# Keys of units 5 to 7 turned to token rows on VectorE instead of TensorE

## The chip, the cores and the metric

The kernel runs on one core of a Trainium2 chip. The metric is the device time of one execution in microseconds (us), taken as the median of several runs.

## The reference

A gated linear attention over 4 batches, 8 heads, 768 tokens and a head width of 48 feeds a three-way maxout layer of 3072 tokens, 384 inputs and 768 hidden features:

```python
f = 1 / (1 + np.exp(-f_logit))
for t in range(S):
    state = f[:, :, t, :, None] * state + np.einsum('bhd,bhe->bhde', k[:, :, t], v[:, :, t])
    y[:, :, t] = np.einsum('bhd,bhde->bhe', q[:, :, t], state)
x = y.transpose(0, 2, 1, 3).reshape(B * S, H * D)
h = np.maximum(np.maximum(x @ w1, x @ w2), x @ w3)
out = h @ w_out
```

Attention inputs are fp32, and the maxout weights come as 64-bit floats, so the kernel converts them to fp32 on the chip.

## The kernel before

**Units.** The sequence is cut into chunks of 64 tokens. A unit u is one chunk of two batches, 128 token rows, so there are 24 units, u = 0 to 23. A head is padded from 48 to 64 features, so two heads fill 128 partitions. For each unit the gates are scanned along the tokens (`scan`, line 316, and `before`, line 334). `after` makes kh, the keys times decay, with features on partitions (line 327), and `before` makes qh (line 338). `pairs` multiplies kh by qh into the PSUM tile a (line 379), and VectorE masks it into at (line 382). `values` multiplies at by v into the PSUM tile y (line 393), and then the keys by v into other columns of the same tile (line 402). For this second product the keys must stand with tokens on partitions, which is the tile ks. VectorE adds the product to the running state (line 410). `finish` adds the part of the older state into y (line 423), and ScalarE copies y to heads (line 429).

**Two ways to ks.** `keys(u)` makes ks with four 128x128 TensorE transposes into a PSUM tile tr (line 354) and one ScalarE copy (line 356). `keys_by_blocks(u, n)` makes one quarter of ks, 32 tokens, with four VectorE transposes that turn 32 by 32 blocks straight from kh to ks (line 369). It is called with n = 0 to 3 for each unit. Before the change, units 0 to 7 (`BY_ROWS = 8`) take the first way and units 8 to 21 the second; the last two units need no ks. The same constant also decides how f, k and q are loaded and turned to features: units 0 to 7 are loaded as token rows and turned by TensorE (line 278), later units are loaded in blocks and turned by VectorE (line 283).

**Maxout stage.** Four units make a group of 512 tokens. `pack` moves their heads to a tile xT by DMA (line 445). `ffn(g, xT)` is a generator. Each step multiplies one block of 128 hidden features by one of the three weights (line 472). The PSUM tile p, which has two buffers, is then read by ScalarE (line 477, for the first weight) or by VectorE (line 479, for the second into top and for the third into hm). After 18 such products come four output products (line 497) and their copies (line 500). A full step takes two turns of `fill`, and its instructions are issued in the first of the two. In the group g = 0, each step also issues conversion work for weights that are needed later: ScalarE (lines 228, 229, 232), then VectorE (line 242), then GpSimd (line 246).

**Order.** The schedule is written by hand. Every engine works through its own list in the order of the program text. `fill(n)` inserts n turns of the generator between the parts of a unit. The main loop runs over u from 4, and the part that matters reads:

```python
fill(...); keys(u); keys_by_blocks(u, 2); finish(u - 1); pairs(u)
sigmoids(u + 1); scan(u + 1)
fill(2); keys_by_blocks(u, 3); after(u + 1); before(u + 1)
fill(2); values(u); carry(u + 1)
fill(1 if u < 2 * GRP else 2)
keys_by_blocks(u + 1, 0)          # and one more fill here for u >= 8
keys_by_blocks(u + 1, 1)
```

Line numbers here and below are those of the profile. SP is the queue that issues nearly all loads and stores; its relevant lines are 182 (block loads), 163 (v), 445 (pack) and 505 (output).

Of the kernel before, what the change touches and what calls it, by code (L numbers as in the profile page):

```python
# [55 lines left out]
def kernel(  # L56
# [15 lines left out]
    NU = B // 2 * (S // C)  # L72
# [5 lines left out]
    GRP = 4  # L78
# [10 lines left out]
    def fast():  # L89
        ctx = ExitStack()  # L90
        with ctx:
# [58 lines left out]
            BY_ROWS = 8  # L150
# [196 lines left out]

            def keys(u):

                if u < min(BY_ROWS, NU - 2):  # L350
                    kh = ready[u]["kh"]
                    tr_s = ps_tr.tile([UT, HP, 128], FP32, name="tr")
                    for hp in range(HP):
                        nc.tensor.transpose(tr_s[:, hp, :], kh[:, hp].rearrange("p a t -> p (a t)"), ident)
                    ks = work.tile([UT, H, DP], FP32, name="ks")
                    nc.scalar.copy(ks.rearrange("s h d -> s (h d)"), tr_s.rearrange("s a d -> s (a d)"))
                    ready[u]["ks"] = ks

            def keys_by_blocks(u, n):

                if BY_ROWS <= u < NU - 2:
                    kh = ready[u]["kh"]
                    if n == 0:
                        ready[u]["ks"] = work.tile([UT, H, DP], FP32, name="ks")
                    ks = ready[u]["ks"].rearrange("s (hp par) d -> s hp par d", par=2)
                    a, t0 = divmod(n * 32, C)
                    for p0 in range(0, 128, 32):
                        par, e0 = divmod(p0, DP)
                        nc.vector.transpose(ks[n * 32:(n + 1) * 32, :, par, e0:e0 + 32], kh[p0:p0 + 32, :, a, t0:t0 + 32])  # L369
# [164 lines left out]
            with tc.manual_schedule():  # L534
# [13 lines left out]
                before(0)  # L548
                sigmoids(1)
                keys(0)  # L550
                scan(1)
                after(1)
# [3 lines left out]
                busy(1)  # L556
                values(0)
                keys(1)
                scan(2)
                after(2)  # L560
# [5 lines left out]
                busy(2)  # L566
                values(1)
                keys(2)
                scan(3)
                after(3)  # L570
# [41 lines left out]
                for u in range(GRP, NU):  # L612
                    n = u + 1
                    fill(0 if u == 2 * GRP else 4 if u % 2 and u > 2 * GRP else 2)
                    keys(u)
                    keys_by_blocks(u, 2)
                    if u > GRP:
                        finish(u - 1)
# [19 lines left out]
                    if CHECKS <= u < CHECKS + len(pieces) // 2:  # L638
                        check_range(2 * (u - CHECKS))
                    fill(2)  # L640
                    keys_by_blocks(u, 3)
                    if n < NU:
                        after(n)
# [13 lines left out]
                    if BY_ROWS <= u + 2 < NU and u % GRP == 0:  # L657
                        load(u + 2, one, "q")
                    keys_by_blocks(n, 0)
                    if u >= 2 * GRP:  # L660
                        fill(2)
# [267 lines left out]
```

## Time and profile before

| | |
|---|---|
| median of 13 runs | 478.95 us (476.82 to 482.94) |
| profiled execution, device time | 481.26 us |
| its span, first to last instruction | 479.6 us |
| TensorE busy | 458.0 us |
| VectorE busy | 269.1 us |
| ScalarE busy | 146.0 us |
| GpSimd busy | 111.1 us |

The span is the part that the trace shows; the profiled execution took 1.66 us more than that and is 2.31 us above the median. In the profile PE is TensorE's matmuls, PEld its weight loads, DVE VectorE, ACT ScalarE, POOL GpSimd. A name such as `tr<-ident,kh` gives the tile written and the tiles read. In the chain of waits each line is a start, a length and a piece of work, all in us.

### The profile page before, as it was taken

What the parts mean: (1) busy time and instruction counts of PE and PEld (TensorE: products, weight loads), DVE (VectorE), ACT (ScalarE), POOL (GpSimd) and SP (SyncE); (2) the same over time, 40 slices, a digit from 0 to 9 for tenths busy, and PEclk for the clock granted to TensorE, in tenths of its full rate; (3) what the DMA queues carried; (4) which work ended last, traced back from release to release, by engine and by line L of the source; (5) the groups of instructions that cost most, each with busy time, mean ns of one, the idle gap of its engine ahead of it and who ended that gap; (6) DMA issues with size and microseconds to landing.
All of it is one profiled execution on the core that took longest, in us unless ns stands there. A gap on an engine that the chain in (4) does not pass through costs nothing.

```text
span 479.6 us, 10276 instructions
## 1 busy us (share of the span) xinstructions
PE 458.0 (96%) x4063; PEld 248.5 (52%) x4063; DVE 269.1 (56%) x528; ACT 146.0 (30%) x343; POOL 111.1 (23%) x134
## 2 busy tenths in 40 slices
PE   4979899999999999999999999999999999999995
PEld 3757645556445445545445544455554445444453
DVE  5965776767487584487685568684674320021110
ACT  2443467522012234144233243242343211100000
POOL 2283644441231230330330311330311300000000
PEclk9987999999999999999999999999999999999999
DMA  9996998614467444576534477524470011200002
GB/s 133 134 287 176 212 347 120 93 49 64 99 95 104 128 81 114 94 138 81 157 77 117 83 139 88 161 62 97 105 146 9 1 51 39 45 1 0 2 17 52
DMA packets 175637, 47.92 MB, mean 100 GB/s; under 512 B 155136, under 2 KB 173184, under 8 KB 175584
## 3 DMA queue, kind: packets, MB, share of 16 engines
q1 hardware_dynamic: 170016, 42.50, 45.8%
q0 software_dynamic: 1008, 3.54, 2.4%
q10 hardware_dynamic: 4560, 1.18, 1.5%
q8 instruction: 33, 0.54, 0.5%
q14 instruction: 20, 0.16, 0.1%
HBM read 37.75 MB, written 4.72 MB: 89 GB/s over the span
## 4 chain that ended last, share of the span: by engine, by line
PE 77%; SPq 8%; DMA 6%; DVE 3%; issue 2%; ACT 2%; ACTq 1%; DVEq 0%
PE p L472 50%; PE p L497 17%; SPq L182 4%; DMA f_ld<-in_f_logit_dram 3%; PE y L423 2%; PE y L393 2%; DMA k_ld<-in_k_dram 2%; PE y L402 2%; SPq L505 2%; PE a L379 2%; DMA raw<-in_moe_w_dram 1%; PE tr L278 1%; SPq L163 1%; DVE r L316 1%; ACTq L445 1%
## 5 line engine op out<-in xcount | busy, mean ns | idle before, releaser
L472 PE MATMUL p<-xT,w_in 128*128 128x512 f32 (+1 forms) x684 | 293.7, 581 | 4.1 <-DVE top L479 2.2
L472 PEld LDWEIGHTS p<-xT,w_in 128*128 128x128 f32 x684 | 128.5, 193 | 139.9 <-issue 127.1
L497 PE MATMUL p<-w_out,hm 128*128 128x384 f32 x288 | 96.3, 489 | 0.0
L479 DVE TENSOR_TENSOR top<-p,top 128x512 f32<-128x512 f32 (+1 forms) x38 | 24.9, 656 | 107.5 <-PE p L472 107.5
L497 PEld LDWEIGHTS p<-w_out,hm 128*128 128x128 f32 x288 | 54.0, 190 | 37.6 <-issue 1.9
L369 DVE STREAM_TRANSPOSE ks<-kh 32x128 f32<-32x128 f32 x224 | 67.7, 302 | 3.6
L477 ACT COPY top<-p 128x512 f32<-128x512 f32 (+1 forms) x38 | 21.3, 562 | 151.4 <-PE p L472 151.4
L326 POOL COPY ends<-r 128x8 f32<-128x8 f32 x24 | 6.9, 288 | 188.2 <-DVE r L316 188.2
L479 DVE TENSOR_TENSOR hm<-p,top 128x512 f32<-128x512 f32 (+1 forms) x38 | 24.7, 651 | 30.5 <-PE p L472 30.5
L429 ACT COPY heads<-y 64x256 f32<-64x256 f32 (+1 forms) x72 | 26.6, 369 | 46.0 <-PE y L423 44.6
L327 POOL TENSOR_TENSOR kh<-kt,r 128x512 f32<-128x512 f32 x16 | 31.4, 1960 | 36.5 <-DVE kt L283 26.1
L500 ACT COPY o<-p 128x384 f32<-128x384 f32 x24 | 11.4, 476 | 86.8 <-PE p L497 83.0
L316 DVE TENSOR_TENSOR_SCAN r<-gate,from_one 128x520 f32<-128x520 f32 x24 | 29.8, 1240 | 9.7 <-ACT gate L295 5.7
L334 DVE TENSOR_TENSOR_SCAN prod<-gate,from_inv 128x520 f32<-128x520 f32 x24 | 31.0, 1291 | 0.0
L246 POOL TENSOR_TENSOR w_in<-top_bits,rest_bits 128x384 uint32<-128x384 uint32 x18 | 19.3, 1076 | 27.5 <-DVE top_bits L242 15.9
L382 DVE TENSOR_TENSOR at<-a,mask 128x512 f32<-128x512 f32 x24 | 16.6, 690 | 11.6 <-PE a L379 11.2
L393 PEld LDWEIGHTS y<-at,v_ld 64*64 64x64 f32 x768 | 13.4, 134 | 15.5 <-issue 9.7
L344 POOL TENSOR_TENSOR state<-st,ends 128x384 f32<-128x384 f32 x22 | 19.8, 901 | 0.1
L338 POOL TENSOR_TENSOR qh<-qt,prod 128x512 f32<-128x512 f32 x16 | 18.8, 1178 | 4.2 <-DVE qt L283 4.2
L283 DVE STREAM_TRANSPOSE gate<-sig 128x512 f32<-128x512 f32 x16 | 11.3, 705 | 15.0 <-ACT sig L298 15.0
L423 PEld LDWEIGHTS y<-qh,state 48*48 48x48 f32 x704 | 11.7, 123 | 13.8 <-issue 11.6
L393 PE MATMUL y<-at,v_ld 64*64 64x64 f32 x768 | 16.7, 224 | 0.0
(79 smaller groups left out, 307.9 us busy)
## 6 DMA issues: line engine op xcount, KB each, us to landing
raw<-in_moe_w_dram SPq DMA_DIRECT2D x27, 384.0 KB, 4.9
v_ld<-in_v_dram SPq DMA_DIRECT2D x48, 96.0 KB, 3.5
raw<-in_moe_w_out_dram SPq DMA_DIRECT2D x12, 384.0 KB, 6.3
out_dram<-o SPq DMA_DIRECT2D x47, 96.0 KB, 2.2
raw<-in_moe_w_dram POOLq DMA_DIRECT2D x9, 384.0 KB, 7.7
xT<-heads SPq DMA_DIRECT2D x30, 72.0 KB, 2.1
f_ld<-in_f_logit_dram SPq DMA_DIRECT2D x32, 64.0 KB, 2.7
k_ld<-in_k_dram SPq DMA_DIRECT2D x32, 64.0 KB, 2.6
```

The source lines that it names most:

```text
L316: nc.vector.tensor_tensor_scan(r[:, 0:LEN][:, ::-1], flat(gate)[:, ::-1], flat(from_one)[:, ::-1], 1.0, op0=ALU.mult, op1=ALU.max)
L327: (nc.vector if u < BY_ROWS else nc.gpsimd).tensor_tensor(kh.rearrange("p h a t -> p a h t"), kt, by_batch(r[:, 1:LEN + 1].rearrange("p (x ...
L334: nc.vector.tensor_tensor_scan(flat(prod), flat(gate_tiles[u % 2]), flat(from_inv[u % 2]), 1.0, op0=ALU.mult, op1=ALU.max)
L344: nc.gpsimd.tensor_tensor(t, states[u % 2], ends[:, u, :].unsqueeze(2).to_broadcast([128, 2 * HP, D]), op=ALU.mult)
L369: nc.vector.transpose(ks[n * 32:(n + 1) * 32, :, par, e0:e0 + 32], kh[p0:p0 + 32, :, a, t0:t0 + 32])
L393: nc.tensor.matmul(y[o:o + DP, a, hp * C:(hp + 1) * C], lhsT=v_ld[s, 2 * hp + par, :], rhs=d["at"][s, par, hp, :], start=(hp == 0), stop=F ...
L423: nc.tensor.matmul(y[o:o + D, a, hp * C:(hp + 1) * C], lhsT=st[r, a, hp, :], rhs=d["qh"][r, a, hp, :], start=False, stop=(hp == HP - 1), s ...
L429: nc.scalar.copy(heads[o, :, t0 + a * C:t0 + (a + 1) * C], y[i, a, 0:HP * C].rearrange("p (h t) -> p h t", h=HP))
L472: nc.tensor.matmul(p if g or w < TOK else p.rearrange("p (two t) -> p two t", two=2), lhsT=w_in[i][:, kt, j * 128:(j + 1) * 128], rhs=rhs, ...
L477: nc.scalar.copy(top, p)
L479: nc.vector.tensor_tensor(hm[:, j, t] if i == 2 else top, p, top, op=ALU.max)
L497: nc.tensor.matmul(p[:, 0:DM], lhsT=hm[:, j, i * UT:(i + 1) * UT], rhs=w_out[:, j, :], start=(j == 0), stop=(j == NJ - 1))
```

## The change

For units 5, 6 and 7 ks is now made by `keys_by_blocks` on VectorE and no longer by `keys` on TensorE and ScalarE. Unit 4 stays as it was, because its first two quarters would be due in the turn u = 3, which the loop does not have. `BY_ROWS` stays 8, so loads and the turning of f, k and q are untouched. GRP is 4 and NU is 24.

```diff
             def keys(u):
 
-                if u < min(BY_ROWS, NU - 2):
+                if u < min(GRP + 1, NU - 2):
                     kh = ready[u]["kh"]
                     tr_s = ps_tr.tile([UT, HP, 128], FP32, name="tr")
...
             def keys_by_blocks(u, n):
 
-                if BY_ROWS <= u < NU - 2:
+                if GRP + 1 <= u < NU - 2:
                     kh = ready[u]["kh"]
                     if n == 0:
                         ready[u]["ks"] = work.tile([UT, H, DP], FP32, name="ks")
```

## The prediction

> **What bounds the kernel now.** I read the busy shares first, then the forms of the two kinds of key transposes.
>
> ```profile
> PE 458.0 (96%) x4063; PEld 248.5 (52%) x4063; DVE 269.1 (56%) x528; ACT 146.0 (30%) x343; POOL 111.1 (23%) x134
> ...
> L354 PE MATMUL tr<-ident,kh 128*128 128x128 f32 x32 | 5.5, 297 | 0.4 <-DVE kh L327 0.4
> ...
> L369 DVE STREAM_TRANSPOSE ks<-kh 32x128 f32<-32x128 f32 x224 | 67.7, 302 | 3.6
> ```
>
> Over the whole span TensorE is the bound and VectorE is little over half busy. Line 354 runs 4 times for each of 8 units; line 369 runs 16 times for each of 14 units. But the change touches only units 5 to 7, so next I read the chain of waits there, and the windows.
>
> ```profile
> 84.77 0.44 PE tr L354 x4
> 85.20 0.59 PE y L423 x32
> 85.80 0.47 PE a L379 x32
> ...
> 108.07 0.52 PE y L402 x31
> ...
> 108.69 0.57 DVE st L410
> ...
> 109.30 0.66 PE y L423 x32
> ```
>
> From 62.65 to 108.59 us the chain holds TensorE alone, and the transposes of units 5, 6 and 7 stand in it at 72.80, 84.77 and 99.30 us, 0.44 us each. At 108.6 it goes over VectorE: finish(7) (line 423) has no product between it and values(7), and waits until line 410 has read the same PSUM tile.
>
> ```profile
> 72.60:84.60 12.00, 12.00 (x163) 6.99 (x162) 8.10 (x13) 8.47 (x18) 4.99 (x6) 1.00 0.80 116
> 84.60:99.10 14.50, 14.50 (x169) 8.13 (x168) 9.51 (x13) 7.55 (x16) 7.59 (x8) 1.00 0.55 77
> 99.10:109.30 10.20, 9.42 (x151) 5.72 (x150) 7.06 (x11) 2.80 (x6) 3.71 (x4) 1.00 0.25 63
> ```
>
> The columns are length, then busy PE, PEld, DVE, ACT, POOL. VectorE is busy 24.67 of these 36.7 us, so only 12.0 us are free. Its waits from 70.2 to 109.3 us are these:
>
> ```profile
> DVE at L382 <- PE a L379: 4.1, 3, 2.4
> DVE r L316 <- ACT gate L295: 4.0, 2, 2.0
> DVE top L479 <- PE p L472: 2.2, 1, 2.2
> DVE st L410 <- PE y L402: 1.3, 1, 1.3
> ```
>
> They are slack: TensorE loses nothing to them except at line 410.
>
> [...] a block transpose moves 32x128 in 302 ns, while line 283 moves 128x512, sixteen times the data, in about 700. [...] scans (two inputs) stretch beside GpSimd, block transposes do not, as the timeline of VectorE shows.
>
> ```profile
> 92.07 1.72 DVE L334 TENSOR_TENSOR_SCAN prod<-gate,from_inv 128x520 f32<-128x520 f32 x1
> ...
> 105.56 1.20 DVE L334 TENSOR_TENSOR_SCAN prod<-gate,from_inv 128x520 f32<-128x520 f32 x1
> ...
> 109.16 3.76 DVE L369 STREAM_TRANSPOSE ks<-kh 32x128 f32<-32x128 f32 x12
> ...
> 121.55 2.50 DVE L369 STREAM_TRANSPOSE ks<-kh 32x128 f32<-32x128 f32 x8
> ```
>
> Twelve take 3.76 us and eight 2.50, both partly beside GpSimd: 0.3125 us from start to start.
>
> **The change part by part.**
>
> *Removed on TensorE:* 3 units x 0.44 us = 1.32 us, all on the path.
>
> *Removed on ScalarE:* 3 copies of 0.58 us (line 356). They stand ahead of the copies to heads and of the next gate, which come about 0.46 us earlier from them and 0.44 from TensorE. ScalarE is off the path, so I price this at nothing by itself; its cover is that TensorE never waits for it here.
>
> *Freed:* one PSUM tile tr per unit. In this stretch line 278 waited for it only once (0.3 us, for the copy of unit 4, which stays). Nothing.
>
> *Added on VectorE:* 3 x 16 = 48 transposes x 0.3125 = 15.0 us, against 12.0 us free. So VectorE fills up and becomes the bound. No DMA and no instruction on SP or POOL is added or moved. Where it is late, POOL is late too (weight sums, line 246; kh and qh of unit 8), and TensorE through at, kh, qh, ks and the two buffers of p.
>
> To see where lateness lands I walk VectorE's list through the new order, each instruction at its start-to-start time in this trace. B8 is two quarters (2.50 us), B4 one (1.25).
>
> Unit 5: line 242 of the step before ends at 71.36; B8 to 73.86; line 242 to 74.32; B4 to 75.57; at (0.69) to 76.26, where it began at 74.37 before. The gate of unit 6 is ready at 76.6, so VectorE idles 0.35 us, its last pause. Then scan and reciprocal 1.39, top 0.57, line 242 twice 0.93: 79.50. B4 to 80.75; kh 0.60, second scan 1.16, qh 0.61, hm 0.60, line 242 0.46, state 0.47: 84.65. TensorE reaches the keys' product (line 402) at 81.1, after ks is whole: no wait.
>
> Unit 6: B8, line 242 (0.50), B4, at: 89.59 instead of 87.02. Scan and reciprocal 1.40, top 0.56, line 242 0.47, B4: ks of unit 6 is whole at 93.27. TensorE, by now 0.88 us ahead, wants it at 92.62 and **waits about 0.7 us**. kh, scan, qh, hm, line 242, state (0.60, 1.16, 0.61, 0.59, 0.47, 0.47): 97.17. hm frees p at about 96.3, just as TensorE wants it.
>
> Unit 7: line 242 blocked by GpSimd as now (1.17), B8, top 0.60, B4, at 0.69, gate, scan and reciprocal 2.15: 105.53. hm ends at about 106.15, when the output product wants it: just in time. B4 to 107.34, then unit 8's kt, scan and qt (0.62, 1.12, 0.68): 109.76. Line 410 runs behind them, to 110.35. So **finish(7) starts at 110.39 instead of 109.30**. GpSimd turns the late kt and qt into qh of unit 8 by 111.28, so pairs(8) starts at 111.33 instead of 109.96: **1.37 us late**, with the 1.32 us of TensorE work already given back.
>
> In this walk the second scans of units 6 and 7 take 1.16 us instead of 1.55 and 1.82, and one line 242 takes 0.50 instead of 1.17, because GpSimd's work no longer falls beside them: 1.72 us less. That is the least certain term. Bounds: all of it comes (the walk), or none of it does, and the result is 1.7 us later. Below the walk there is little: the counted instructions have no slack left but 0.35 us. I take the walk.
>
> *What is absorbed:* at 141.3 TensorE waits about 0.45 us for q of unit 10, at the end of a row of SP issues that runs without a break from 101 us, begun by heads(6), which the change does not delay. A late TensorE does not meet this wait: 1.37 - 0.45 = +0.92 us. Later stretches over SP and ScalarE (183, 264 us) start from TensorE's own results, so the rest passes through to the end.
>
> Span 479.6 + 0.92 = 480.5; with the 1.66 us around it the profiled execution would be 482.2. That execution is 2.31 us above the median, so against the median: 478.95 + 0.92 = **479.9 us**.
>
> **The rivals.**
>
> *A, GpSimd's relief does not come* (slower): VectorE, full from 76.6 us on, pays the contended times. Line 410 of unit 7 then ends near 112, and finish(7) and pairs(8) with it: +0.92 + 1.72 = +2.6, 481.6 us. It decides for slower as soon as 0.5 us more than in the walk falls on VectorE. For it: all pauses are used up, so each such delay counts fully. Against: scans outside this stretch do run at 1.12.
>
> *B, VectorE hides everything*: -1.32, 477.6 us. It needs the 48 transposes to fit into 12.0 us, so 0.25 us each; no row shows them so short.
>
> *C, the gain is made and lost at 141 us*: if VectorE costs nothing and SP's row does not move, TensorE arrives early and waits: 478.95. That SP's row starts from heads(6), which would be earlier too, speaks against it.
>
> That the change does nothing is excluded by the code: for units 5 to 7 all four quarter calls exist, and unit 4 keeps its own way.
>
> **How the numbers follow.** A difference under 0.3%, or 1.44 us, is about what a measurement of this kernel cannot tell from none. Walk: 0.50 (of which 0.08 ends above 480.4, 0.42 within). A: 0.35, slower. C: 0.08, same. B: 0.07, since -1.32 lies just inside the bound, 0.02 same and 0.05 faster with a little help. Faster 0.05, same 0.52, slower 0.43. The range 478.0 to 482.0 leaves out most of B, and the upper part of A where new contention joins.
>
> **What would show it.** Right: VectorE without pauses from 76 to 110 us; line 382 of unit 6 near 89; a TensorE wait of under 1 us for ks of unit 6 near 93; finish(7) near 110.4 after a wait for line 410 of about 2.4 us (0.7 before); line 356 five times, line 369 272 times. Wrong: pauses of VectorE left in unit 7 (B or C), second scans of units 6 and 7 still at 1.5 to 1.8 us or finish(7) after 111.5 (A), or a long TensorE wait at the p buffers, which in the walk come free just in time.

## The result and the profile after

The changed kernel takes 483.01 us (median of 11 runs, 480.26 to 484.47), the kernel before 479.16 us in the same comparison (48 runs). The recorded ratio is 1.0072, with a 95% interval of 1.0049 to 1.0094: slower by 3.4 us (2.3 to 4.5). The two medians are 3.85 us apart, which lies within that interval. Slower is the side that 0.43 was given to; 483.01 us lies above the predicted 479.9 us and above the range of 478.0 to 482.0. The profiled execution took 483.89 us, with a span of 482.2.

The page of the changed kernel, busy times and the granted TensorE clock in tenths, and then the clock on the page of before:

```profile
PE 458.5 (95%) x4051; PEld 247.3 (51%) x4051; DVE 282.9 (59%) x576; ACT 144.6 (30%) x340; POOL 107.6 (22%) x134
...
PEclk9988999997999999999999999999999999999999
```

```profile
PEclk9987999999999999999999999999999999999999
```

VectorE has its 48 instructions more and 13.8 us more work. The new thing is the 7 in the tenth slice (108.5 to 120.5 us), where the page of before has a 9. The low third and fourth slices stand in both. The windows of the changed kernel, columns as before:

```profile
72.60:84.60 12.00, 11.25 (x150) 6.14 (x138) 11.52 (x25) 8.45 (x19) 3.65 (x5) 1.00 0.82 116
84.60:99.10 14.50, 14.23 (x164) 7.77 (x164) 14.00 (x31) 6.32 (x14) 5.50 (x7) 1.00 0.52 72
99.10:109.30 10.20, 9.43 (x147) 5.27 (x146) 9.79 (x23) 2.22 (x5) 2.00 (x4) 1.00 0.28 68
```

VectorE is now busy 35.31 of 36.7 us. Of its waits from 70.2 to 109.3 us none is left: the only one that the view lists for this window, 0.7 us ahead of hm, was over at 69.79 us. TensorE waits instead. Its timeline in the changed kernel (start, length, line, idle time ahead and what ended it):

```profile
84.70 0.66 PE L423 MATMUL y<-qh,state 48*48 48x64 f32 x32 [0.85 <-DVE st L410]
...
93.35 0.66 PE L402 MATMUL y<-v_ld,ks 64*64 64x48 f32 x26 [0.17 <-DVE ks L369]
...
110.69 0.66 PE L423 MATMUL y<-qh,state 48*48 48x64 f32 x32 [2.17 <-DVE st L410]
111.76 1.13 PE L379 MATMUL a<-qh,kh 48*64 48x64 f32 x32 [0.40 <-POOL qh L338]
112.82 10.70 PE L497 MATMUL p<-w_out,hm 128*128 128x384 f32 x24
```

These are finish(5), the key product of unit 6, finish(7), pairs(8) and the two output products behind it. The same last three in the kernel before:

```profile
109.30 0.66 PE L423 MATMUL y<-qh,state 48*48 48x64 f32 x32 [0.78 <-DVE st L410]
109.78 0.65 PE L379 MATMUL a<-qh,kh 48*64 48x64 f32 x32
110.36 8.01 PE L497 MATMUL p<-w_out,hm 128*128 128x384 f32 x24
```

The waits at finish(5), at the key product and at finish(7) are VectorE's lateness. The lengths of the last two lines are something else: pairs(8) took 0.65 us and the two output products 8.01, here 1.13 and 10.70. The windows of the changed kernel show why. After PEld, DVE, ACT and POOL, the third number from the end is the granted clock:

```profile
110.70:111.70 1.00, 0.66 (x32) 0.51 (x32) 0.96 (x4) 0.28 (x1) 1.00 (x2) 0.88 0.03 2
111.70:113.00 1.30, 1.24 (x33) 1.12 (x34) 1.25 (x5) 0.83 (x3) 0.80 (x2) 0.50 0.00 0
...
117.00:118.00 1.00, 1.00 (x3) 0.50 (x2) 0.96 (x2) 0.00 (x0) 0.00 (x0) 0.50 0.68 86
118.00:119.00 1.00, 1.00 (x4) 0.63 (x3) 0.94 (x3) 0.00 (x0) 0.19 (x1) 0.86 0.55 64
```

From about 111.5 to 118.3 us TensorE got half its clock.

To compare stages, I take starts from the timelines of TensorE, counted from values(4) (its first line 393), because the stretch from the start to values(4) takes 64.2 to 67.4 us in the fourteen profiles, whatever the kernel. Each column is the time from the point before it:

| profile of | values(4), from start | to finish(7) | to pairs(8) | to values(8) | to finish(8) | to finish(11) | to finish(15) | to finish(19) |
|---|---|---|---|---|---|---|---|---|
| before | 66.31 | 42.99 | 0.48 | 8.52 | 12.87 | 50.64 | 72.80 | 74.30 |
| before, again (e12) | 64.88 | 42.99 | 0.48 | 8.52 | 12.87 | 50.73 | 72.99 | 72.02 |
| changed | 65.83 | 44.86 | 1.07 | 11.69 | 12.87 | 50.16 | 72.47 | 72.60 |
| changed, again (e5) | 66.57 | 44.87 | 1.07 | 10.07 | 12.87 | 50.16 | 72.04 | 72.11 |

So the change makes TensorE 1.87 + 0.59 = **2.46 us late** at pairs(8), the same in both executions. The clock adds 3.17 us in one and 1.55 in the other. About 0.5 us comes back before finish(11), where TensorE no longer waits for a load.

### The profile page after: what moved, and what is told of

Same layout as the page of the kernel before. It is cut to its first block, busy times and chain, and to the rows that moved or that the text cites. A ratio compares the mean times of both kernels' runs of the same rounds, so it can differ in the third digit from the quotient of the medians.

```text
span 482.2 us, 10295 instructions
## 1 busy us (share of the span) xinstructions
PE 458.5 (95%) x4051; PEld 247.3 (51%) x4051; DVE 282.9 (59%) x576; ACT 144.6 (30%) x340; POOL 107.6 (22%) x134
## 4 chain that ended last, share of the span: by engine, by line
PE 82%; DVE 7%; DMA 5%; issue 2%; SPq 1%; POOL 1%; ACT 0%; DVEq 0%; ACTq 0%; POOLq 0%
PE p L472 52%; PE p L497 20%; DMA k_ld<-in_k_dram 2%; PE y L393 2%; PE y L423 2%; PE a L379 2%; PE y L402 2%; DVE r L316 2%; DVE ks L369 1%; DVE prod L334 1%; SPq L182 1%; DMA f_ld<-in_f_logit_dram 1%; DMA q_ld<-in_q_dram 1%; POOL kh L327 1%; DMA raw<-in_moe_w_dram 1%
## 5 line engine op out<-in xcount | busy, mean ns | idle before, releaser
L497 PE MATMUL p<-w_out,hm 128*128 128x384 f32 x288 | 99.2, 500 | 0.0
L369 DVE STREAM_TRANSPOSE ks<-kh 32x128 f32<-32x128 f32 x272 | 82.2, 302 | 4.4
L497 PEld LDWEIGHTS p<-w_out,hm 128*128 128x128 f32 x288 | 55.2, 195 | 39.4 <-issue 5.2
L326 POOL COPY ends<-r 128x8 f32<-128x8 f32 x24 | 5.6, 233 | 191.6 <-DVE r L316 191.6
L246 POOL TENSOR_TENSOR w_in<-top_bits,rest_bits 128x384 uint32<-128x384 uint32 x18 | 18.3, 1018 | 26.7 <-DVE top_bits L242 16.1
L393 PEld LDWEIGHTS y<-at,v_ld 64*64 64x64 f32 x768 | 13.4, 134 | 15.5 <-issue 10.2
L283 DVE STREAM_TRANSPOSE gate<-sig 128x512 f32<-128x512 f32 x16 | 11.3, 705 | 13.8 <-ACT sig L298 13.8
L423 PE MATMUL y<-qh,state 48*48 48x64 f32 x704 | 14.6, 221 | 3.7 <-DVE st L410 3.7
```

The source lines that it names most:

```text
L393: nc.tensor.matmul(y[o:o + DP, a, hp * C:(hp + 1) * C], lhsT=v_ld[s, 2 * hp + par, :], rhs=d["at"][s, par, hp, :], start=(hp == 0), stop=F ...
L423: nc.tensor.matmul(y[o:o + D, a, hp * C:(hp + 1) * C], lhsT=st[r, a, hp, :], rhs=d["qh"][r, a, hp, :], start=False, stop=(hp == HP - 1), s ...
L497: nc.tensor.matmul(p[:, 0:DM], lhsT=hm[:, j, i * UT:(i + 1) * UT], rhs=w_out[:, j, :], start=(j == 0), stop=(j == NJ - 1))
```

## The experiments

**Theories.** *Clock*: the loss is VectorE's lateness plus a fall of the granted clock that TensorE's pauses at finish(7) and pairs(8) bring about. *Lateness alone*: the fall is chance, or belongs to something else, and the lateness accounts for the loss. A second question is where the lateness comes from: VectorE filled up (15.0 us into 12.0), or each moved unit costing by itself. The table gives each run against the kernel before on the same chip, with the mean granted clock of its runs. The clock of the kernel before is 0.9915 in the sets of e1 to e8 and 0.9910 in that of e9 to e12. In the first comparison only the 13 executions of the changed kernel have clocks on record, so their 0.9876 can be set only against the later sets.

By estimate 0.001 of mean clock is 0.5 us (0.001 x 480). But the mean takes in the whole span. In all fourteen profiles TensorE is also slow between 30 and 42 us: the windows show 0.50 from 32 to 41 us in the kernel before and 0.52 from 33 to 40 in the changed one, and in the others two products of 128x256 take 1.19 us there, or sixteen to nineteen take 5.29 to 7.49, where e12 has two in 0.70 just before and the kernel before has twelve in 2.75 at a clock of 1.00. Behind the last product, where it costs no time, the windows have 0.79 from 478.0 to 479.5 us in the kernel before and 0.52 from 480.0 to 482.2 in the changed one. So small differences of the mean say little, and only profiles show where the clock falls.

| run | ratio, 95% interval | mean clock | values(4) to finish(7), us |
|---|---|---|---|
| changed, first comparison | 1.0072 (1.0049 to 1.0094) | 0.9876 | 44.86 |
| e5 changed, again | 1.0072 (1.0051 to 1.0092) | 0.9885 | 44.87 |
| e1 changed, pause filled | 1.0053 (1.0027 to 1.0078) | 0.9918 | 44.87 |
| e2 before, 9 more on VectorE | 1.0040 (1.0022 to 1.0058) | 0.9890 | 44.40 |
| e3 before, 8 fillers on TensorE | 1.0028 (1.0009 to 1.0048) | 0.9926 | 45.80 |
| e8 before, 15 more on VectorE | 1.0091 (1.0068 to 1.0113) | 0.9860 | 46.40 |
| e4 changed, output product moved | 1.0089 (1.0056 to 1.0123) | 0.9865 | 46.70 |
| e6 units 5 and 6 only | 1.0034 (1.0020 to 1.0048) | 0.9920 | 43.68 |
| e7 unit 7 only | 1.0033 (1.0019 to 1.0047) | 0.9896 | 43.01 |
| e9 changed, VectorE lightened | 0.9997 (0.9976 to 1.0018) | 0.9907 | 41.95 |
| e10 before, VectorE lightened | 0.9987 (0.9963 to 1.0012) | 0.9914 | 42.99 |
| e11 before, one filler | 0.9984 (0.9967 to 1.0001) | 0.9917 | 42.99 |

### e1: the changed kernel with the pause filled

`busy(n)` issues n filler products whose result nobody reads (line 523); the kernel before already has such products in its first units.

```diff
+                    if u == 2 * GRP:
+                        busy(4)
                     if u > GRP:
                         finish(u - 1)
```

> The changed kernel, with four filler products (line 523, result unused, about 2.1 us) on TensorE between values(7) and finish(7), where it would wait for VectorE. Clock theory: the 2.2 us wait made the granted clock fall to 0.50 for about 7 us, which cost 3.1 us; with TensorE kept busy the clock stays at 1.00, finish(7) and pairs(8) start as in the changed kernel (within 0.3 us), the two output products behind them take 8.0 us instead of 10.7, and the time is 0 to 1 us above the kernel before (ratio 1.000 to 1.002). Lateness theory: the loss comes from VectorE's late results alone and the clock was chance; the time stays where the changed kernel is, 1.005 to 1.009.

The timeline of TensorE in e1:

```profile
108.84 1.99 PE L523 MATMUL p<-from_one,ident 128*128 128x256 f32 x8
111.08 0.66 PE L423 MATMUL y<-qh,state 48*48 48x64 f32 x32 [0.24 <-DVE st L410]
112.15 0.69 PE L379 MATMUL a<-qh,kh 48*64 48x64 f32 x32 [0.41 <-POOL qh L338]
112.77 8.01 PE L497 MATMUL p<-w_out,hm 128*128 128x384 f32 x24
```

The filler stands where the pause was. finish(7) and pairs(8) come as late after values(4) as in the changed kernel (44.87 and 1.07 us), yet the output products are back at 8.01 us, and the mean clock over twelve runs is that of the kernel before. So the clock follows the pause and not the late data. The time is 1.0053, outside the 1.000 to 1.002 that I expected of the clock theory and just inside the 1.005 to 1.009 written for lateness alone. The first range had taken off 2 us for a wait at 288 us that turned out to be chance (e12). Lateness without any fall of the clock, 2.46 - 0.5 = 2.0 us, is 1.004, inside the interval. By times e1 and the changed kernel are not apart, since their intervals overlap; it is the clock that differs.

### e5: the changed kernel again

No edit.

> The changed kernel once more, unaltered, to see how often and where the granted clock falls. Clock theory: the mean granted clock of its runs lies below that of the kernel before by 0.003 to 0.004 (1.5 to 2 us of 480), the drop lies behind the wait at finish(7), and the time is 2.3 us of lateness plus that, ratio 1.006 to 1.010. Lateness alone: the mean clocks are equal and the ratio is about 1.005, as with the filler in e1_warm.

The waits repeat to 0.01 us, and the clock falls at the same place, for a shorter time. TensorE in e5:

```profile
112.51 1.13 PE L379 MATMUL a<-qh,kh 48*64 48x64 f32 x32 [0.40 <-POOL qh L338]
113.58 9.07 PE L497 MATMUL p<-w_out,hm 128*128 128x384 f32 x24
```

Within this set the clock of the six runs is 0.0030 below before, 1.4 us. Over the 19 runs of the changed kernel it is 0.0036 below the same value, 1.7 us, as expected, and the ratio is 1.0072 again.

### e2, e8 and e3: the kernel before made late by pausing and by working

In e2 and e8, n = 9 and 15 unused block transposes go ahead of line 410 of unit 7; in e3 eight fillers go ahead of finish(7), as in e1.

```diff
+                    if u == 2 * GRP - 1:
+                        scratch = work.tile([128, PIECE], FP32, name="top_bits", bufs=4)
+                        scratch = scratch[0:32, 0:128].rearrange("p (x t) -> p x t", t=32)
+                        for i in range(n):
+                            nc.vector.transpose(scratch, ready[u]["kh"][0:32, :, 0, 0:32])
                     values(u)
```

> The kernel before, with nine more VectorE block transposes (line 369's kind, into an unused tile, 2.8 us) between unit 8's qt and the state of unit 7 (line 410); keys still by TensorE. This makes TensorE wait about 2.2 us at finish(7) instead of 0.7 and changes nothing else. Clock theory: the granted clock falls to 0.5 for about 7 us, TensorE is 1.5 + 3.1 = 4.6 us late at 123 us, of which about 2.4 us is absorbed later; time +2 us or more, ratio 1.004 to 1.007. Lateness theory: +1.5 us at most, clock at 1.00, ratio 1.000 to 1.003.

> The kernel before, with eight filler products (about 4.2 us, result unused) on TensorE between values(7) and finish(7). TensorE is late by 4.2 - 0.7 = 3.5 us there without having paused. Absorption theory: TensorE waits 0.45 us near 141 and 2.0 us near 288 us for loads anyway, and both waits shrink by what it is late: time +1.0 us, ratio 1.001 to 1.003, with the wait near 288 us gone. Pass-through, as the prediction had it: 3.5 - 0.45 = +3.0 us, ratio 1.006. In both the clock stays at 1.00.

> The kernel before, with fifteen more VectorE block transposes (4.7 us, into an unused tile) between unit 8's qt and line 410 of unit 7. TensorE waits about 4.0 us at finish(7), so it is about 3.4 us late there, as late as with the eight fillers of e3_busy8, but idle instead of working. Clock theory: the granted clock falls to 0.5 for some us in most runs, mean clock lower than before by 0.004 or more, time above e3_busy8's by about 3 us: ratio 1.009 to 1.013. Lateness alone: same as e3_busy8 within its interval plus the difference in lateness, ratio 1.003 to 1.006, clock as before.

The windows of e8, which waited 4.18 us at finish(7), and then those of e3:

```profile
108.00:114.00 6.00, 1.82 (x82) 1.28 (x84) 5.51 (x19) 0.48 (x1) 2.71 (x3) 1.00 0.32 60
114.00:118.00 4.00, 4.00 (x68) 2.67 (x58) 3.83 (x12) 1.10 (x3) 0.00 (x0) 0.57 0.04 10
```

```profile
108.00:114.00 6.00, 6.00 (x84) 4.44 (x83) 3.79 (x12) 1.11 (x3) 0.00 (x0) 1.00 0.21 28
114.00:118.00 4.00, 4.00 (x13) 2.31 (x13) 1.73 (x2) 1.00 (x2) 0.00 (x0) 1.00 0.47 70
```

TensorE is 3.41 us late at finish(7) in e8 and 2.81 in e3, nearly the same. But in e8 it had paused, and its clock was then 0.57 on average from 114 to 118 us; in e3 it had worked, and it stayed at 1.00. Over all runs the mean clocks are 0.9860 and 0.9926, a difference of 3.2 us, and the times differ by 1.0091 - 1.0028 = 0.0063, 3.0 us, of which 0.6 is the lateness. That is as the clock theory expected and outside the range of lateness alone. Not all of it need belong to finish(7): in e8's profile the fall there costs 1.7 us (0.43 of 4 us), and at least 1.4 us was lost long before the added work, behind a wait of 2.71 us for a load of q: the 24 products from 52.71 us on took 7.03 us, where the kernel before takes 2.75 and 2.86 for twelve each.

e2 is the middle case. With one wait of 2.19 us the profiled execution lost no clock there:

```profile
110.48 0.67 PE L423 MATMUL y<-qh,state 48*48 48x64 f32 x32 [2.19 <-DVE st L410]
110.97 0.65 PE L379 MATMUL a<-qh,kh 48*64 48x64 f32 x32
111.55 8.01 PE L497 MATMUL p<-w_out,hm 128*128 128x384 f32 x24
```

Yet over 22 runs its mean clock is 0.0024 below before, 1.2 us. So my expectation of a sure fall was wrong. That such a wait brings the clock down in other executions is what the mean suggests, and isn't shown: in this profile too the 24 products from 51.45 us on took 7.03 us, behind a wait of 2.64 us for a load of q.

e3 also asked whether lateness is absorbed later. Its 1.3 us (0.4 to 2.3) agrees with 2.81 less the 0.5 us before finish(11) only at the upper end; its clock, 0.0012 above before, would account for another 0.5 us. A further absorption near 288 us isn't shown: e3 waited there, although it came late.

### e12: the kernel before again

No edit.

> The kernel before, a second look. If the 2.0 us wait for a load near 288 us in its first profile is chance, it is gone or differs by more than 0.5 us here, and the stretch from finish(15) to finish(19) takes 72.0 us instead of 74.3; the stretch from values(4) to finish(7) repeats at 43.0 us.

In the first profile of before TensorE had this wait:

```profile
288.82 5.42 PE L472 MATMUL p<-xT,w_in 128*128 128x512 f32 x12 [2.01 <-DVE top L479]
```

In the second one it is gone (72.02 us from finish(15) to finish(19) instead of 74.30), and 42.99 repeats exactly. Of the fourteen profiles only this one and that of e3 (1.63 us) have it. The wait is chance, and the kernel before usually has nothing to give back there. The first profile of before was, at 481.26 us, one of its slower executions, partly for this.

### e6 and e7: part of the change

`keys` and `keys_by_blocks` select units 5 and 6 (e6) or unit 7 (e7):

```diff
-                if u < min(BY_ROWS, NU - 2):
+                if u < min(BY_ROWS, NU - 2) and u not in (5, 6):
...
-                if BY_ROWS <= u < NU - 2:
+                if (BY_ROWS <= u or u in (5, 6)) and u < NU - 2:
```

> Only units 5 and 6 turn their keys on VectorE; unit 7 stays on TensorE. VectorE gets 10.0 us more against 12.0 us free. Fill-up theory: VectorE catches up in unit 7, line 410 of unit 7 runs as soon as TensorE is done, the wait at finish(7) is 0.7 us as before, TensorE saves 0.9 us and loses about as much waiting for VectorE at finish(5) and for ks of unit 6: ratio 0.998 to 1.002. Rival, each unit costs its share: two thirds of the change's loss, ratio 1.004 to 1.006.

> Only unit 7 turns its keys on VectorE; units 5 and 6 stay on TensorE. VectorE gets 5.0 us more where it has 2.2 + 0.8 + 0.7 + 1.3 = 5.0 us of pauses. Fill-up theory: line 410 of unit 7 ends at most 0.5 us later than before, the wait at finish(7) stays near 1 us, TensorE saves 0.44 us: ratio 0.998 to 1.002. Rival, the place decides (unit 7 stands just ahead of the one exposed wait): nearly the whole loss, ratio 1.004 to 1.007.

Both are slower by some 1.6 us, which is in neither of the two ranges written for each. The profiles say more. In e6 VectorE does catch up and the wait at finish(7) is 0.78 us as before. But measured from start to start, TensorE loses 0.93 us at finish(5), 0.49 at the key product of unit 6 (of which the view lists 0.17 as a wait) and 0.16 in the maxout products behind it, against the 0.88 us of transposes saved: +0.69 us at finish(7). That is half of its loss, and the clock is as before. The other half may lie behind it: to finish(8) this profile takes 13.16 us instead of 12.87 and to finish(11) 51.51 instead of 50.64, with a wait of 1.07 us behind the load of q near 142 us. One profile doesn't show whether that is chance. In e7:

```profile
107.99 0.67 PE L423 MATMUL y<-qh,state 48*48 48x64 f32 x32 [1.23 <-DVE st L410]
109.06 0.69 PE L379 MATMUL a<-qh,kh 48*64 48x64 f32 x32 [0.40 <-POOL qh L338]
```

The 0.44 us saved goes into these two waits (+0.61 at pairs(8)), and the mean clock is 0.0019 lower, 0.9 us. Neither part is a gain: neither units 5 and 6 together nor unit 7 alone find room on VectorE whose use does not delay TensorE.

### e9 and e10: VectorE lightened

```diff
-                    else:
+                    elif n < 16:
                         nc.vector.scalar_tensor_tensor(top, hi, 3, top, op0=ALU.logical_shift_left, op1=ALU.bitwise_xor)
```

> The changed kernel without line 242 for weight pieces 16 to 23: eight conversions on VectorE, about 4.4 us in the stage of units 5 to 7, are left out, so these weights are not converted. To be read against e10_light_before. Fill-up theory: VectorE now has 15.0 us more to do against 12.0 + 4.4 = 16.4 us free, so it keeps up; the wait at finish(7) goes back to about 1 us, the stretch from values(4) to finish(7) is no more than 0.3 us longer than in e10, the clock stays up, and the ratio is 0.997 to 1.001 of e10. Rival, moving the transposes costs by itself (waits of the single unit, small instructions): the stretch is still more than 1 us longer than in e10 and the time 1.003 or more of it.

> The kernel before without line 242 for weight pieces 16 to 23, the base for e9_light_change: those weights are not converted. VectorE is off TensorE's path there except at finish(7), so all theories expect the time of the kernel before, ratio 0.998 to 1.001.

With room on VectorE the change does what it was moved for: from values(4) to finish(7) TensorE needs 41.95 us instead of 42.99, 1.04 of the 1.32 us of transposes. VectorE's waits from 62 to 112 us in e9 are back:

```profile
DVE r L316 <- ACT gate L295: 2.3, 2, 1.6
DVE hm L479 <- PE p L472: 0.7, 1, 0.7
DVE top L479 <- PE p L472: 0.5, 1, 0.5
```

So the 1.87 us at finish(7) in the changed kernel come from VectorE being full. pairs(8) still waits for qh, and of the 1.04 us 0.45 is left there:

```profile
106.54 0.67 PE L423 MATMUL y<-qh,state 48*48 48x64 f32 x32 [0.99 <-DVE st L410]
107.61 0.98 PE L379 MATMUL a<-qh,kh 48*64 48x64 f32 x32 [0.40 <-POOL qh L338]
```

In this execution even these two short waits were followed by a fall of the clock (0.71 from 107 to 109 us, 0.50 from 109 to 111), which I had expected to stay up. The time does not tell e9 from e10 (0.9997 and 0.9987, both intervals over 0.002 to either side): what TensorE gains is not seen at the end.

### e4: an output product ahead of finish(7)

```diff
-                    fill(0 if u == 2 * GRP else 4 if u % 2 and u > 2 * GRP else 2)
+                    fill(4 if u % 2 and u > 2 * GRP else 2)
...
-                    fill(2)
+                    fill(0 if u == 2 * GRP else 2)
                     keys_by_blocks(u, 3)
```

> The changed kernel, with the second output product (line 497, 4.0 us) of group 0 moved from behind pairs(8) to ahead of finish(7), so that TensorE works while VectorE finishes line 410. Clock theory: no wait of TensorE at finish(7), clock 1.00, about 2.2 + 0.4 us of waits and 3.1 us of low clock saved against the changed kernel, part of which is lost again in the waits for loads near 141 and 288 us: at or a little below the kernel before, ratio 0.997 to 1.001. Lateness theory: VectorE's lateness moves on to pairs(8) or values(8), ratio above 1.003.

The wait at finish(7) is hidden, but finish(7) comes 3.7 us later than in the kernel before, behind the product. ScalarE then copies to heads late, issues its part of `pack`, and makes the gate of unit 9 late; VectorE waits 3.24 us for it, and the last quarter of ks of unit 8 stands behind that. TensorE in e4:

```profile
120.29 0.31 PE L402 MATMUL y<-v_ld,ks 64*64 64x48 f32 x2 [2.85 <-DVE ks L369]
120.95 1.09 PE L402 MATMUL y<-v_ld,ks 64*64 64x48 f32 x26 [0.34 <-DVE ks L369]
```

A somewhat longer pause in a new place, and the clock falls there (1.09 us for 26 products, 5.20 instead of 4.14 for the output product behind it). It is slower than before by 0.9%, in the range written for lateness alone, though the clock fell too: the wait had only moved.

### e11: a filler in the kernel before

`busy(1)` at the place of e1, in the kernel before.

> The kernel before with one filler product (0.5 us, result unused) in the 0.7 us wait at finish(7). If a wait of 0.7 us already costs clock in some runs, the mean clock rises by 0.001 or more and the time falls, ratio 0.997 to 0.999; if only longer waits do, the same time, 0.999 to 1.001.

Ratio 0.9984 (0.9967 to 1.0001), clock 0.0007 above before. The interval just reaches 1, so whether the short pause of the kernel before costs clock stays open. It is the only variant that may be faster than both kernels, and it isn't shown to be.

## Why the prediction was wrong, point by point

- **The gain, 1.32 us of TensorE.** Right in the main. It shows as soon as VectorE has room: 1.04 us in e9.
- **VectorE fills up, and finish(7) pays.** Right in mechanism and place: no pause on VectorE after 76 us, line 382 of unit 6 at 88.88, the wait at finish(7) 2.17 us where 2.4 was written. e9 confirms the cause. Some of this agreement is luck: this execution reached values(4) 0.48 us earlier than the one that the walk was made from, so counted from there line 382 came 0.46 us late. The length of the wait is near because TensorE came about 1.0 us later than walked and line 410 about 0.8. hm was not quite in time: the twelve output products that end with it took 4.26 us instead of 4.03.
- **The size of the lateness.** Too small: 1.37 us at pairs(8), and 2.46 was measured. Some 0.9 us is the walk itself: the handovers at both ends of each group of transposes, which the walk took at nothing or at the overlap of other pairs, took 0.03 to 0.13 us more, and the second scans 1.33 us from start to start instead of 1.16. Another 0.18 us was a slip of views: the old start of pairs(8) was read from the chain of waits (109.96), where the timeline has 109.78. The walk also overlooked finish(5), which waits for line 410 of unit 5 for the same reason as finish(7); it cost little in the end, as VectorE was the bound by then, and unit 6's ks cost 0.5 us instead of 0.7.
- **GpSimd's relief.** Most of it came: from start to start 1.28 of the 1.72 us, in the two scans and in one line 242. VectorE's timeline in the changed kernel has the scans of units 6 and 7 at 1.23 us, where they took 1.45 and 1.72 before:

```profile
81.00 1.23 DVE L334 TENSOR_TENSOR_SCAN prod<-gate,from_inv 128x520 f32<-128x520 f32 x1
...
87.00 0.56 DVE L242 SCALAR_TENSOR_TENSOR top_bits<-raw,top_bits 128x384 uint32<-128x384 uint32 x1
...
93.93 1.23 DVE L334 TENSOR_TENSOR_SCAN prod<-gate,from_inv 128x520 f32<-128x520 f32 x1
```

  So rival A, which came nearest in time (481.6 us), fell by its mechanism. Before, GpSimd's line 246 ran from 91.69 to 92.68 us when the scan began at 92.07, and the scan took 1.72 us; in the changed kernel line 246 was over at 93.11 when the scan began at 93.93, and the scan took 1.23. The scan of 1.20 us that the prediction shows at 105.56 us was not free of GpSimd, as the prediction took it to be: line 327 began beside it at 105.78, and there GpSimd was the second to come. So not every overlap stretched a scan, and what decides it isn't shown.
- **What is absorbed.** Right for this change: 0.45 us was said for the wait near 141 us, and the stretch up to finish(11) went from 50.64 to 50.16 us. It is no fixed amount, for in e2 TensorE came 1.4 us late and still took 50.93.
- **The term that was left out: the clock.** This is the larger of the two steps that failed; the other is the lateness above, too small by 1.1 us. The prediction priced a wait of TensorE at its length and put the clock at nothing, although the page of before has it down in the third and fourth slice, next to pauses of 1.71 and 0.48 us. Behind the pauses at finish(7) and pairs(8) the clock went to half for several us: this cost 3.17 and 1.55 us in the two profiles, and by the mean clocks 1.7 us on average over 19 runs. With the pause at finish(7) filled it stayed up (e1: the two output products in 8.01 us, a mean clock of 0.9918). Nor did it take a long pause: waits of 2.17 and 0.40 us were followed by half clock for 6.8 us (111.5 to 118.3) in the first profile of the changed kernel and for 3.4 in e5, and waits of 0.99 and 0.40 us for 3.4 in e9. In e2 no fall came behind a wait of 2.19 us. Why so short a pause is enough, and why not in every execution, isn't shown.

Sum by the measured terms: 2.46 late, less 0.5 absorbed, plus 1.7 of clock is 3.7 us, against 3.4 (2.3 to 4.5) in the times. The forecast of 0.92 lacks both: 1.1 of lateness and 1.7 of clock.

## What to carry to other kernels

Before moving work from a bound engine to one that looks half idle, count the pauses of the second engine in that very stage: 15.0 us did not fit into 12.0, although VectorE was idle 44% of the whole span. Price a new wait of TensorE above its length, for the clock may fall behind it, as it did here behind 2.17 and 0.40 us, and compare the mean granted clocks of many executions, since single profiles differ: the fall cost 3.17 us in one of the changed kernel and 1.55 in the other. A wait that one profile shows for a load may be chance, like the 2.01 us near 288 us that e12 did not have: read a second profile of the same kernel before counting on it to absorb anything.

## What was not expected of the hardware

Short pauses of TensorE were followed by half clock in some executions and not in others. From finish(7) to values(8), seven of the fourteen profiles have waits of 1.39 to 4.18 us in sum, and in five of them the clock falls there (both of the changed kernel, e8 and e9 by their windows, e4 by the lengths of its products), in two not (e2, e7: the two output products in 8.01 us). The other seven wait 0.78 us at most, and none falls (8.01 us again). A single wait of 2.01 us near 288 us in the kernel before left the clock at 1.00 too.

The mean clocks go the same way: 2.17 and 0.40 us lowered it by 0.0036 over 19 runs, 4.18 us by 0.0055 over six, though in e8 not all of that need come from this pause. Filling the pause with products of no use kept the clock at that of the kernel before (0.9918 against 0.9915). By the windows, the stretches at half clock lasted 3.4 us in e5, e8 and e9, 6.8 at both places in the changed kernel, and 10.2 from 31.7 to 42.0 us in the kernel before; behind the pause they cost 1.55 us in e5 and 3.17 in the first profile of the changed kernel.
